# Recurrent-memory layer: another order of the model dimension, a fold of fewer products, output heads in column pieces, and a last step without queries

## The chip, the cores and the metric

The kernel runs on one core of one Trainium2 chip. The metric is the device time of one execution of the program in microseconds, as the median of several runs.

The core's engines work side by side, each through its own queue in a fixed order: TensorE (PE; its weight loads are shown as PEld), VectorE (DVE), ScalarE (ACT), GpSimd (POOL) and SyncE (SP), whose queue issues the DMA transfers here. An engine waits for another through semaphores.

## The reference

The prompt is 2048 tokens of 640 features. Four layers run one after the other, A, B, A, B, each with a layer norm before it and its result added to the residual x. Layer A is attention in four segments of 512 tokens with a linear memory (32 heads of 20). Layer B is a recurrent memory transformer with 32 heads of 128: 64 segments of 32 tokens, each with 8 memory tokens ahead of it.

```python
def _B_ref(x, mem0, Wq, Wk, Wv, Wo, seg_len):
    B, S, Dm = x.shape                 # 1, 2048, 640
...
    mask = (idx[:, None] < M) | (idx[:, None] >= idx[None, :])
    mem = mem0
    outs = []
    for s in range(n_seg):
        xs = x[:, s * seg_len:(s + 1) * seg_len, :].copy()
        h = jnp.concatenate([mem, xs], axis=1)
        q = jnp.einsum('btd,dhe->bhte', h, Wq)
        k = jnp.einsum('btd,dhe->bhte', h, Wk)
        v = jnp.einsum('btd,dhe->bhte', h, Wv)
        scores = jnp.einsum('bhqe,bhke->bhqk', q, k) * scale
        scores = jnp.where(mask[None, None], scores, -1000000000.0)
        p = _softmax(scores, axis=-1)
        o = jnp.einsum('bhqk,bhke->bhqe', p, v)
        o = jnp.einsum('bhte,hed->btd', o, Wo)
        mem = o[:, :M, :].copy()
        outs.append(o[:, M:, :])
    return jnp.concatenate(outs, axis=1)
...
x = A_x
x = x + _A_ref(_layernorm(x, axis=-1), A_wq, A_wk, A_wv, A_wo, A_beta)
x = x + _B_ref(_layernorm(x, axis=-1), B_mem0, B_Wq, B_Wk, B_Wv, B_Wo, B_seg_len)
x = x + _A_ref(_layernorm(x, axis=-1), A_wq, A_wk, A_wv, A_wo, A_beta)
x = x + _B_ref(_layernorm(x, axis=-1), B_mem0, B_Wq, B_Wk, B_Wv, B_Wo, B_seg_len)
return x
```

The memory of a segment is the output of the eight memory tokens of the segment before, so the 64 segments of a layer B are a chain. The eight memory rows that the last segment puts out are not returned.

## The kernel before

The residual lies in DRAM twice: in f32 (`xres`) and rounded to bf16 (`xres_bf`, from which layer B's layer norms read). The weights of layer B stay in SBUF with the model dimension on the 128 partitions in five chunks of 128 rows: `b_wq` and `b_wk` for the whole program, `b_wv` and `b_wo` for a layer.

Layer A (`layer_A`) goes through four segments of four 128-token tiles. The last thing it does for a tile is to store the new residual (L380), to round it (`a_xnb`; L383 on ACT in the last segment, L385 on POOL in the others) and to store that (L386). The first step's work of the next layer B, its layer norms and its first tail units, follows.

Layer B (`layer_B`) runs the 64 segments as steps. Every instruction of TensorE, ScalarE, VectorE and GpSimd is recorded through a helper, so that the profile shows L109 for all of them, and each engine keeps the order in which the program is written. A step has 32 columns that depend on the chain, eight memory rows and the first 24 tokens of the next segment, in the tile `HX` (`cols_of`); the eight last tokens of the segments, the tails, are worked off ahead of their steps in larger pieces, as filler between the chain's pieces. A step s does, in this order:

- `thin_mm`: the projections `b_Ka`, `b_Qa`, `b_Kb`, `b_Qb` (a and b are halves of the heads) of the 32 columns. The 32 columns are the stationary operand; four column groups of 32 of the PE array run at once, each on 512 other columns of the weight, five chunks deep. So a projection is 20 matmuls. Their results go to `b_kq` (ACT and DVE).
- `transp4` (`b_TPak`, `b_TPaq`, `b_TPbk`, `b_TPbq`) turns them, and they are scattered to the tiles `KT` and `QT`: the memory's part to those of this step, the part of the 24 tokens to those of the next.
- `mask_mm` and `scores` to `b_SP`, softmax on DVE and ACT (and POOL for one half), and turns of P on DVE. Under it PE does `b_Va` and `b_Vb`, a layer norm's transposes when one is due, and a unit of tail projections (`tail_unit`, `b_tail`). In the last steps of a layer that have no tail left, the unit is a repetition whose result is not used.
- `pv`: P times V to `b_OTP`, evicted to `b_OTsb` by ACT and DVE.
- `od_chunk(0)`: half of a chunk of deferred output heads of the tails (`b_OPSd`), then the output heads of the step with `o_mm` to `b_OPS`: the four column groups hold two heads times two halves of the 640 output columns, 320 columns each. That makes 16 rounds of four matmuls, in groups of two rounds by the list `order`. Then `od_chunk(1)`.
- the fold, which brings the memory rows from `b_OPS` to the memory columns of `HX` that the next projections use. ACT copies `b_OPS` to `b_msb` in three parts (64, 128, 128 columns); for each part PE multiplies slices of 32 columns of `b_msb`, as the stationary operand, with the constant `b_sel` (`selm`, 8 columns), which picks the memory rows, adds the two heads' groups and turns them (`b_MT`); DVE copies `b_MT` to `HX`. Between the parts lie chunks of `b_vtail` (`vtail_some`), values of tails of later steps, five chunks of four matmuls of 256 columns in a step.
- `x_out`: DVE adds `b_OPS` to the residual rows `b_XO`, and SP stores them (`store_head`, L1052). The residual rows were loaded at the step's start (L1102). The tails' residual (`b_XOd`, and `b_XOe` for the last four steps) is loaded and stored by `tail_dma` (L1063, L1061).

For the fold, a half jj of the output columns holds, of each chunk of 128 columns of the model dimension, the 64 columns of that half (`wo_half`, `d_half`):

```python
def wo_half(h, jj2):
    return W.wo[:, h, :].rearrange("p (c j x) -> p j c x", j=2, x=64)[:, jj2]

def d_half(rows, jj2):
    return rows.rearrange("t (c j x) -> t j c x", j=2, x=64)[:, jj2]
```

so that a chunk c of the next projections needs the columns 64c to 64c+63 of `b_OPS` in all four groups. One chunk takes four products, one for each column group of the result, over two slices of 32 columns and the two heads' halves of `b_sel`. The loads and stores of residual rows move pieces of 64 columns, 256 bytes, by the same rule.

The lines that the change and the prediction touch, besides these: L228 loads a weight of the next layer A (`a_wkv`) from its copy in DRAM; L760 and L765 load `b_wq`, `b_wk` and `b_wv`; L999 loads the first memory.

Of the kernel before, what the change touches and what calls it, by code (L numbers as in the profile page):

```python
# [18 lines left out]
F32 = mybir.dt.float32  # L19
# [10 lines left out]
NCH = 5  # L30
# [215 lines left out]
def layer_A(nc, tc, C, W, x_src, x_dst, src_is_bf16, nseg=4, out_bf16=False, xb_dst=None, load_w=None, side_loads=None):  # L246
# [7 lines left out]
    with ExitStack() as ctx:  # L254
# [105 lines left out]
        def out_stage_b(n_, tt, halves=(0, 1)):  # L360
            d = SEG[n_]
            oT, xr = d["oT"][tt], d["xr"][tt]
            r0 = n_ * 512 + tt * 128
            if xr is None:
                xr = wkl.tile([128, D], BF16 if src_is_bf16 else F32, name="a_xr")
                nc.sync.dma_start(xr[:], x_src[r0:r0 + 128, :])
            if n_ == nseg - 1 and (tt or not src_is_bf16):
                d["xnew"] = up.tile([128, D], F32, name="a_xnew", tag="PT") if tt else xr
            elif 0 in halves:
                d["xnew"] = w1l.tile([128, D], F32, name="a_xnew") if src_is_bf16 else xr  # L370
            xnew = d["xnew"]
            for half in halves:
                YP = pg.tile([128, 320], F32, name="a_YP", tag="pg")
                for c in range(NCH):
                    nc.tensor.matmul(YP[:], lhsT=oT[:, c, :], rhs=W.wo[:, c, 320 * half:320 * half + 320],
                                     start=(c == 0), stop=(c == NCH - 1))
                C.after2 = K("xnew").vector.tensor_tensor(out=xnew[:, 320 * half:320 * half + 320], in0=YP[:], in1=xr[:, 320 * half:320 * half + 320], op=ALU.add)
            if 1 not in halves:
                return
            nc.sync.dma_start(x_dst[r0:r0 + 128, :], xnew[:])  # L380
            xnb = w1l.tile([128, D], BF16, name="a_xnb")
            if n_ == nseg - 1:
                nc.scalar.copy(xnb[:], xnew[:])  # L383
            else:
                K("xnb").gpsimd.tensor_copy(xnb[:], xnew[:])  # L385
            nc.sync.dma_start(xb_dst[r0:r0 + 128, :], xnb[:])  # L386

        GS = {}
# [362 lines left out]
    return W  # L751


def load_B_resident(nc, W, B_Wq, B_Wk, k, after):

    c, r = divmod(k, 8)
    t, src = ((W.wk, B_Wk), (W.wq, B_Wq))[r % 2]
    h = r // 2
    nc.gpsimd.tensor_copy(t[0:1, c, 1024 * h:1024 * h + 1], after[0:1, 0:1])
    nc.sync.dma_start(t[:, c, 1024 * h:1024 * h + 1024], src[128 * c:128 * c + 128, 8 * h:8 * h + 8].rearrange("p h e -> p (h e)"))  # L760


def load_B_wv(nc, W, B_Wv):
    for c in range(NCH):
        nc.sync.dma_start(W.wv[:, c, :], B_Wv[128 * c:128 * c + 128].rearrange("p h e -> p (h e)"))  # L765


def load_B_wo(nc, W, B_Wo, k):
# [9 lines left out]
def layer_B(nc, tc, C, W, x_src, xb_src, x_dst, mem0, B_Wv, B_Wo, nsteps=64, out_bf16=False, tag=""):  # L778
# [8 lines left out]
    with ExitStack() as ctx:  # L787
# [21 lines left out]
        def ps_tile(shape, dtype, name):  # L809
            return pp.tile(shape, dtype, name=name, tag="ps")  # L810
# [68 lines left out]
        def thin_mm(cols_ap, Wt, b, name):  # L879
            ps = ps_tile([128, 512], F32, name)  # L880
            for c in range(NCH):
                for j in range(4):
                    n = 4 * b + j
                    nc.tensor.matmul(ps[32 * j:32 * j + 32, :], lhsT=cols_ap[:, c, :], rhs=Wt[:, c, 512 * n:512 * n + 512],
                                     start=(c == 0), stop=(c == NCH - 1), tile_position=(0, 32 * j), skip_group_check=True)
            return ps

        def transp4(sb, name, tp=None):
            if tp is None:
                tp = ps_tile([128, 4, 128], BF16, name)  # L890
            for i in range(4):
                nc.tensor.transpose(tp[:, i, :], sb[:, 128 * i:128 * i + 128], C.identb[:])
            return tp
# [76 lines left out]
                dma(VTd[8 * T:8 * T + 8, :, o:o + 256].rearrange("s t f -> (s t) f"), vt[64 * jj:64 * jj + 64])  # L970

        def wo_half(h, jj2):
            return W.wo[:, h, :].rearrange("p (c j x) -> p j c x", j=2, x=64)[:, jj2]

        def d_half(rows, jj2):
            return rows.rearrange("t (c j x) -> t j c x", j=2, x=64)[:, jj2]

        def o_mm(ops_, src_ap_fn, hpairs, first, last):
            for n_, h0 in enumerate(hpairs):
                for e in range(2):  # L980
                    for jj2 in range(2):
                        k = 2 * e + jj2
                        nc.tensor.matmul(ops_[32 * k:32 * k + 32, :].rearrange("p (c x) -> p c x", x=64), lhsT=src_ap_fn(h0 + e), rhs=wo_half(h0 + e, jj2),
                                         start=(first and n_ == 0), stop=(last and n_ == len(hpairs) - 1),
                                         tile_position=(0, 32 * k), skip_group_check=True)

# [9 lines left out]
        nc.gpsimd.memset(HX[0][:, :, 0, 0:8], 0.0)  # L996
        with nc.allow_non_contiguous_dma(reason="mem0 transpose load (tiny)"):
            for c in range(NCH):
                nc.sync.dma_start(HX[0][:, c, 1, 0:8], mem0[:, 128 * c:128 * c + 128].rearrange("t p -> p t"))  # L999
        tu_homes = ((kqp, "kq"),) * 4 + ((w2, "QT"), (w2, "KT"), (wk, "tu"), (w2, "Vth"))  # L1000
        for k in range(16):
            tail_unit(0, k, shared=True)
# [46 lines left out]
        def store_head(s):  # L1049
            def f(xo):  # L1050
                for jj2 in range(2):
                    nc.sync.dma_start(d_half(x_dst[32 * s:32 * s + 24, :], jj2), xo[32 * jj2:32 * jj2 + 24, :].rearrange("t (c x) -> t c x", x=64))  # L1052
            return f

        def tail_dma(s0, store, xo):
            x_ = x_dst if store else x_src
            for jj2 in range(2):
                sb = xo[32 * jj2:32 * jj2 + 32, :].rearrange("t (c x) -> t c x", x=64)
                dr = x_[32 * s0:32 * s0 + 128, :].rearrange("(i t) (c j x) -> i t j c x", t=32, j=2, x=64)[:, 24:32, jj2]
                if store:  # L1060
                    nc.sync.dma_start(dr, sb)  # L1061
                else:
                    nc.sync.dma_start(sb, dr)  # L1063
# [25 lines left out]
        for s in range(nsteps):  # L1089
# [9 lines left out]
                if s % 2:  # L1099
                    tl = tails_load(s + 1)  # L1100
            for jj2 in range(2):
                nc.sync.dma_start(XO[32 * jj2:32 * jj2 + 24, :].rearrange("t (c x) -> t c x", x=64), d_half(x_src[32 * s:32 * s + 24, :], jj2))  # L1102

            def x_scatter(tp, b, D_):
                if not last:
# [57 lines left out]

            Ka = thin_mm(cols, W.wk, 0, "b_Ka")
            ka = kq(Ka, "act")
            Qa = thin_mm(cols, W.wq, 0, "b_Qa")
            qa = kq(Qa, "dve", SCB)
            Kb = thin_mm(cols, W.wk, 1, "b_Kb")
            kb = kq(Kb, "act")
            Qb = thin_mm(cols, W.wq, 1, "b_Qb")  # L1170
            qb = kq(Qb, "act", SCB)

            TPak = transp4(ka, "b_TPak")
            scatter("dve", TPak, 0, KT[s], 0, 8, 32)
            x_scatter(TPak, 0, KT)
            TPaq = transp4(qa, "b_TPaq")
            scatter("dve", TPaq, 0, QT[s], 0, 8, 24)
            x_scatter(TPaq, 0, QT)
# [4 lines left out]
            TPbq = transp4(qb, "b_TPbq", po.tile([128, 4, 128], BF16, name="b_TPbq", tag="tail"))  # L1183
            scatter("dve", TPbq, 1, QT[s], 0, 8, 24)
            x_scatter(TPbq, 1, QT)
            SPb = mask_mm(1)
            scores((SPa, SPb))
            for f in (soft_max, soft_sub, soft_exp):
# [190 lines left out]
```

## Time and profile before

| | |
|---|---|
| runs, us | 2589.53, 2586.01, 2582.91 (median 2586.01) |
| the profiled execution: its time, us | 2585.25 |
| its span, first to last instruction, us | 2583.5 |
| granted TensorE clock | 0.996 |
| the two layers B, 63 steps each, us | 885.3 and 882.6 |
| period of a step, median, us | 13.98 |
| a projection of 20 matmuls, us | 1.08 |
| `b_OPS`, 64 matmuls, us | 2.17 |
| last rounds of `b_OPS` to the next `b_Ka`, median, us | 1.18 |
| ACT copy `b_msb` of 64 and 128 columns, mean ns | 213 (first part), 277 |

The page's busy times say how long an engine worked in the whole span. The chain of waits goes back from the last instruction to what released each, and its shares say on which engine the end hung. "issue" is time in which an engine waited for nothing that the profile shows. Matmuls are pipelined: in the timeline a group's time includes the overlap with the next one, and a round's cost is read from the distance of the starts. A line of the timeline gives start, time, engine, line, operation, output and inputs, the tile's shape and the count; in brackets stand the idle time of the engine before it and what ended it.

### The profile page before, as it was taken

To read this page: it belongs to the slowest core of one execution; us is meant where nothing else is said; L and a number is where in the kernel's file an instruction comes from. 1 tells how busy PE (TensorE), PEld (TensorE's weight loads), DVE (VectorE), ACT (ScalarE), POOL (GpSimd) and SP (SyncE) were. 2 spreads that over 40 slices of the span, in tenths; PEclk is the share of its full clock that TensorE was granted. 3 is DMA by queue.
4 is the path that set the end of the run, shared out by engine and by line. 5 is a ranking of instruction groups with operands and counts; after the bars stand their busy time and mean duration, and the time that the engine had idled before them with its cause. 6 is when DMAs were issued, how large, how long until landed. Compare 5 with 4: busy or idle time off the path is not lost.

```text
span 2583.5 us, 139561 instructions
## 1 busy us (share of the span) xinstructions
PE 2482.8 (96%) x62024; PEld 1637.5 (63%) x62088; DVE 1704.5 (66%) x4738; ACT 1521.3 (59%) x3430; POOL 704.9 (27%) x1515
## 2 busy tenths in 40 slices
PE   7999999999999999999979899999999999999998
PEld 5556576666666666666655566766666666666665
DVE  8999855565556555555579998555655565565555
ACT  6988945555555545444369889455555555555443
POOL 6677621111111111111146776211111111111110
PEclk9999999999999999999999999999999999999999
DMA  4122272222222222121220112822212122211111
GB/s 158 45 84 73 83 245 51 48 47 46 46 50 48 46 50 43 40 39 30 61 85 17 63 50 55 265 47 47 44 42 47 42 46 43 46 43 35 38 26 21
DMA packets 325309, 157.19 MB, mean 61 GB/s; under 512 B 244960, under 2 KB 309600, under 8 KB 322912
## 3 DMA queue, kind: packets, MB, share of 16 engines
q1 hardware_dynamic: 324704, 148.26, 22.1%
q8 instruction: 485, 7.95, 1.3%
q14 instruction: 120, 0.98, 0.1%
HBM read 96.46 MB, written 51.71 MB: 57 GB/s over the span
## 4 chain that ended last, share of the span: by engine, by line
PE 77%; DVE 14%; ACT 6%; issue 2%; DMA 1%; POOL 0%; SPq 0%; ACTq 0%; DVEq 0%; POOLq 0%
PE b_OPS L109 11%; DVE a_nm L138 6%; PE b_Ka L109 5%; PE b_Qb L109 5%; PE b_Kb L109 5%; PE b_Qa L109 5%; PE b_tail L109 5%; PE b_SP L109 4%; PE b_Va L109 4%; PE b_Vb L109 4%; PE b_vtail L109 3%; PE b_OPSd L109 3%; ACT a_PT L138 3%; PE b_OTP L109 3%; PE a_S L109 2%
## 5 line engine op out<-in xcount | busy, mean ns | idle before, releaser
L109 PEld LDWEIGHTS <-b_HX 128*32 128x32 bf16 x15360 | 428.7, 96 | 329.5 <-DVE b_HX L109 0.5
L109 POOL TENSOR_TENSOR b_Pn<-b_E,b_rs 128x200 bf16<-128x200 bf16 x128 | 78.2, 611 | 1334.4 <-PE b_Vb L109 893.7
L138 DVE TENSOR_REDUCE a_nm<-a_S 128x2 f32<-128x512 f32 (+3 forms) x512 | 395.0, 816 | 34.7 <-PE a_S L109 26.4
L138 ACT ACTIVATE a_PT<-a_T 128x1024 bf16<-128x1024 f32 (+1 forms) x384 | 344.3, 901 | 32.8 <-PE a_T L109 25.0
L109 PE MATMUL b_OPS<-b_wo,b_OTsb 128*32 128x320 bf16 x8192 | 302.4, 299 | 1.8 <-issue 0.8
L109 PEld LDWEIGHTS <-b_OTsb 128*32 128x32 bf16 x8192 | 204.4, 96 | 77.2 <-DVE b_OTsb L109 3.1
L138 POOL TENSOR_SCALAR_AFFINE_SELECT a_PT<-a_PT 128x256 bf16<-128x256 bf16 x380 | 188.6, 505 | 129.8 <-ACT a_PT L138 128.4
L109 DVE CAST b_HX<-b_MT 128x8 bf16<-128x8 f32 x372 | 63.9, 172 | 232.3 <-PE b_MT L109 226.6
L109 ACT CAST b_msb<-b_OPS 128x64 bf16<-128x64 f32 x378 | 69.4, 256 | 222.1 <-PE b_OPS L109 222.0
L109 ACT CAST b_kq<-b_Kb 128x512 bf16<-128x512 f32 x128 | 75.0, 586 | 200.4 <-PE b_Kb L109 200.4
L109 DVE COPY b_KT<-b_TPak 128x128 bf16<-128x128 bf16 x128 | 28.8, 225 | 228.1 <-PE b_TPak L109 228.1
L109 DVE TENSOR_SCALAR b_kq<-b_Qa 128x512 bf16<-128x512 f32 x128 | 88.6, 692 | 120.0 <-PE b_Qa L109 116.7
L109 PE MATMUL b_Va<-b_wv,b_HX 128*32 128x512 bf16 x2520 | 161.1, 380 | 0.0
L109 PE MATMUL b_Vb<-b_wv,b_HX 128*32 128x512 bf16 x2520 | 160.9, 379 | 0.0
L109 PEld LDWEIGHTS <-b_kq 128*128 128x128 bf16 x2080 | 116.8, 98 | 68.9 <-ACT b_kq L109 55.6
L109 PE MATMUL b_Ka<-b_wk,b_HX 128*32 128x512 bf16 x2520 | 158.3, 378 | 0.0
L109 PE MATMUL b_Qa<-b_wq,b_HX 128*32 128x512 bf16 x2520 | 158.2, 379 | 0.0
L109 PE MATMUL b_Qb<-b_wq,b_HX 128*32 128x512 bf16 x2520 | 158.2, 379 | 0.0
L109 PE MATMUL b_Kb<-b_wk,b_HX 128*32 128x512 bf16 x2520 | 158.2, 379 | 0.0
L109 DVE CAST b_OTsb<-b_OTP 128x160 bf16<-128x160 f32 (+1 forms) x384 | 131.0, 377 | 35.0 <-PE b_OTP L109 28.9
L109 PEld LDWEIGHTS <-c_identb 128*128 128x128 bf16 x1240 | 102.2, 98 | 60.1 <-issue 29.4
L109 ACT CAST b_kq<-b_Ka 128x512 bf16<-128x512 f32 x128 | 75.0, 586 | 108.8 <-PE b_Ka L109 108.8
(206 smaller groups left out, 5502.4 us busy)
## 6 DMA issues: line engine op xcount, KB each, us to landing
b_QKd<-b_tu SPq DMA_DIRECT2D x128, 128.0 KB
b_tl<-b_QKd SPq DMA_DIRECT2D x64, 256.0 KB
b_wv<-in_B_Wv_dram SPq DMA_DIRECT2D x10, 1024.0 KB
b_wo<-in_B_Wo_dram SPq DMA_DIRECT2D x16, 640.0 KB
b_Vth<-b_VTd SPq DMA_DIRECT2D x512, 16.0 KB
b_XO<-xres SPq DMA_DIRECT2D x256, 30.0 KB
b_VTd<-b_vt SPq DMA_DIRECT2D x224, 32.0 KB
b_xt<-xres_bf SPq DMA_DIRECT2D x40, 160.0 KB
```

Source lines behind the costliest of these rows:

```text
L109: r = f(*a, **k)
L138: r = f(*a, **k)
```

## The change

Layer B keeps the model dimension in another order. Chunks 0 to 3 take 128 rows each: chunk c takes the rows 320 (c mod 2) + 128 (c div 2) and the following; chunk 4 takes the rows 256 to 319 and 576 to 639. The weights `b_wq`, `b_wk` and `b_wv` and the first memory are loaded in this order, and layer A writes `xres_bf` in it, with two copies to `a_xnb` (512 and 128 columns) for the one there was: both on POOL, and in the last segment one on ACT and one on DVE. The halves of the output columns thereby become contiguous, 0 to 319 and 320 to 639, in `b_wo` and in the loads and stores of residual rows.

With this order the 128 columns of a part of `b_msb` serve two chunks, one for each half. A product takes a slice of 32 columns and all 16 columns of `b_sel`, and gives eight memory columns for either chunk. The parts are 128, 128 and 64 columns wide (64, 128, 128 before); there are 4 + 4 + 4 products (4 + 8 + 8 before), the last four with 8 columns. One chunk of `b_vtail` stands ahead of them (two before), two behind the first group (one before).

The last group of `b_OPS` is computed in two column pieces, 0 to 127 and 128 to 319: 8 + 8 matmuls for 8.

In the last step of a layer B the memory tokens' queries, whose outputs nobody reads, are left out: no `b_Qa`, `b_Qb`, no `b_TPaq`, `b_TPbq`, and POOL sets those columns of `QT` to zero.

```diff
@@ layer_A
             xnb = w1l.tile([128, D], BF16, name="a_xnb")
-            if n_ == nseg - 1:
-                nc.scalar.copy(xnb[:], xnew[:])
-            else:
-                K("xnb").gpsimd.tensor_copy(xnb[:], xnew[:])
+            halves_ = xnew[:].rearrange("p (j x) -> p j x", j=2)
+            moves = ((xnb[:, 0:512].rearrange("p (b j k) -> p b j k", b=2, j=2), halves_[:, :, 0:256].rearrange("p j (b k) -> p b j k", b=2)),
+                     (xnb[:, 512:640].rearrange("p (j k) -> p j k", j=2), halves_[:, :, 256:320]))
+            for (dst, src), last_ in zip(moves, (nc.scalar.copy, nc.vector.tensor_copy)):
+                (last_ if n_ == nseg - 1 else K("xnb").gpsimd.tensor_copy)(dst, src)
             nc.sync.dma_start(xb_dst[r0:r0 + 128, :], xnb[:])
@@
+def b_rows(src, c):
+
+    if c == 4:
+        return src.rearrange("(j k) h e -> j k h e", k=320)[:, 256:320]
+    o = 320 * (c % 2) + 128 * (c // 2)
+    return src[o:o + 128]
@@ load_B_resident, load_B_wv
-    nc.sync.dma_start(t[:, c, 1024 * h:1024 * h + 1024], src[128 * c:128 * c + 128, 8 * h:8 * h + 8].rearrange("p h e -> p (h e)"))
+    nc.sync.dma_start(t[:, c, 1024 * h:1024 * h + 1024], b_rows(src, c)[..., 8 * h:8 * h + 8, :].rearrange("... h e -> ... (h e)"))
-        nc.sync.dma_start(W.wv[:, c, :], B_Wv[128 * c:128 * c + 128].rearrange("p h e -> p (h e)"))
+        nc.sync.dma_start(W.wv[:, c, :], b_rows(B_Wv, c).rearrange("... h e -> ... (h e)"))
@@ layer_B
         def wo_half(h, jj2):
-            return W.wo[:, h, :].rearrange("p (c j x) -> p j c x", j=2, x=64)[:, jj2]
+            return W.wo[:, h, 320 * jj2:320 * jj2 + 320]
         def d_half(rows, jj2):
-            return rows.rearrange("t (c j x) -> t j c x", j=2, x=64)[:, jj2]
-        def o_mm(ops_, src_ap_fn, hpairs, first, last):
+            return rows[:, 320 * jj2:320 * jj2 + 320]
+        def o_mm(ops_, src_ap_fn, hpairs, first, last, c0=0, c1=320):
...
-                        nc.tensor.matmul(ops_[32 * k:32 * k + 32, :].rearrange("p (c x) -> p c x", x=64), lhsT=src_ap_fn(h0 + e), rhs=wo_half(h0 + e, jj2),
+                        nc.tensor.matmul(ops_[32 * k:32 * k + 32, c0:c1], lhsT=src_ap_fn(h0 + e), rhs=wo_half(h0 + e, jj2)[:, c0:c1],
@@ first memory
-                nc.sync.dma_start(HX[0][:, c, 1, 0:8], mem0[:, 128 * c:128 * c + 128].rearrange("t p -> p t"))
+                for p0, n_ in ((0, 64), (64, 64)) if c == 4 else ((0, 128),):
+                    o = 256 + 5 * p0 if c == 4 else 320 * (c % 2) + 128 * (c // 2)
+                    nc.sync.dma_start(HX[0][p0:p0 + n_, c, 1, 0:8], mem0[:, o:o + n_].rearrange("t p -> p t"))
@@ tail_dma; store_head and the load of b_XO likewise
-                sb = xo[32 * jj2:32 * jj2 + 32, :].rearrange("t (c x) -> t c x", x=64)
-                dr = x_[32 * s0:32 * s0 + 128, :].rearrange("(i t) (c j x) -> i t j c x", t=32, j=2, x=64)[:, 24:32, jj2]
+                sb = xo[32 * jj2:32 * jj2 + 32, :]
+                dr = x_[32 * s0:32 * s0 + 128, :].rearrange("(i t) d -> i t d", t=32)[:, 24:32, 320 * jj2:320 * jj2 + 320]
@@ a step
-            Qa = thin_mm(cols, W.wq, 0, "b_Qa")
-            qa = kq(Qa, "dve", SCB)
+            if not last:
+                Qa = thin_mm(cols, W.wq, 0, "b_Qa")
+                qa = kq(Qa, "dve", SCB)
...
-            Qb = thin_mm(cols, W.wq, 1, "b_Qb")
-            qb = kq(Qb, "act", SCB)
+            if last:
+                nc.gpsimd.memset(QT[s][:, :, 24:32], 0.0)
+            else:
+                Qb = thin_mm(cols, W.wq, 1, "b_Qb")
+                qb = kq(Qb, "act", SCB)
...
-                o_mm(ops, lambda h: OTsb[:, 40 * h + 8:40 * h + 40], [16 * a + 4 * j + 2 * ip for ip in range(2)], n_ == 0, n_ == 7)
+                for c0, c1 in ((0, 128), (128, 320)) if n_ == 7 else ((0, 320),):
+                    o_mm(ops, lambda h: OTsb[:, 40 * h + 8:40 * h + 40], [16 * a + 4 * j + 2 * ip for ip in range(2)], n_ == 0, n_ == 7, c0, c1)
...
-            vtail_some(2)
+            vtail_some(1)
...
-                parts = ((0, 1), (1, 3), (3, NCH))
+                parts = ((0, 128), (128, 256), (256, 320))
                 for ca, cb in parts:
-                    nc.scalar.copy(msb[:, 64 * ca:64 * cb], ops[:, 64 * ca:64 * cb])
+                    nc.scalar.copy(msb[:, ca:cb], ops[:, ca:cb])
                 for pi, (ca, cb) in enumerate(parts):
-                    mt = ps_tile([128, cb - ca, 8], F32, f"b_MT{pi}")
-                    for c in range(ca, cb):
-                        for q in range(4):
-                            o = 64 * c + 32 * (q % 2)
-                            nc.tensor.matmul(mt[32 * q:32 * q + 32, c - ca, :], lhsT=msb[:, o:o + 32], rhs=selm[:, q // 2, :],
-                                             start=True, stop=True, tile_position=(0, 32 * q), skip_group_check=True)
-                    nc.vector.tensor_copy(dst[:, ca:cb, 0:8], mt[:])
-                    vtail_some((1, 1, NCH)[pi])
+                    mt = ps_tile([128, 2, 8] if pi < 2 else [128, 8], F32, f"b_MT{pi}")
+                    for q in range(4):
+                        o = ca + 32 * q if pi < 2 else ca + 32 * (q % 2)
+                        nc.tensor.matmul(mt[32 * q:32 * q + 32], lhsT=msb[:, o:o + 32], rhs=selm[:] if pi < 2 else selm[:, q // 2, :],
+                                         start=True, stop=True, tile_position=(0, 32 * q), skip_group_check=True)
+                    nc.vector.tensor_copy(dst[:, 2 * pi:2 * pi + 2, 0:8] if pi < 2 else dst[:, 4, 0:8], mt[:])
+                    vtail_some((2, 1, NCH)[pi])
```

More of the change, by code (lines that the diff above doesn't have):

```diff
@@ L1051, in f @@
                 for jj2 in range(2):
-                    nc.sync.dma_start(d_half(x_dst[32 * s:32 * s + 24, :], jj2), xo[32 * jj2:32 * jj2 + 24, :].rearrange("t (c x) -> t c x", x=64))
+                    nc.sync.dma_start(d_half(x_dst[32 * s:32 * s + 24, :], jj2), xo[32 * jj2:32 * jj2 + 24, :])
             return f
@@ L1101, in layer_B @@
             for jj2 in range(2):
-                nc.sync.dma_start(XO[32 * jj2:32 * jj2 + 24, :].rearrange("t (c x) -> t c x", x=64), d_half(x_src[32 * s:32 * s + 24, :], jj2))
+                nc.sync.dma_start(XO[32 * jj2:32 * jj2 + 24, :], d_half(x_src[32 * s:32 * s + 24, :], jj2))
             def x_scatter(tp, b, D_):
@@ L1175, in layer_B @@
             x_scatter(TPak, 0, KT)
-            TPaq = transp4(qa, "b_TPaq")
-            scatter("dve", TPaq, 0, QT[s], 0, 8, 24)
-            x_scatter(TPaq, 0, QT)
+            if not last:
+                TPaq = transp4(qa, "b_TPaq")
+                scatter("dve", TPaq, 0, QT[s], 0, 8, 24)
+                x_scatter(TPaq, 0, QT)
             TPbk = transp4(kb, "b_TPbk")
@@ L1182, in layer_B @@
             SPa = mask_mm(0)
-            TPbq = transp4(qb, "b_TPbq", po.tile([128, 4, 128], BF16, name="b_TPbq", tag="tail"))
-            scatter("dve", TPbq, 1, QT[s], 0, 8, 24)
-            x_scatter(TPbq, 1, QT)
+            if not last:
+                TPbq = transp4(qb, "b_TPbq", po.tile([128, 4, 128], BF16, name="b_TPbq", tag="tail"))
+                scatter("dve", TPbq, 1, QT[s], 0, 8, 24)
+                x_scatter(TPbq, 1, QT)
             SPb = mask_mm(1)
```

## The prediction

> **What bounds the kernel now.** I read the page's busy times first, then the chain that ended last, then the timeline of one fold, then the chain at the ends of the layers.
>
> ```profile
> PE 2482.8 (96%) x62024; PEld 1637.5 (63%) x62088; DVE 1704.5 (66%) x4738; ACT 1521.3 (59%) x3430; POOL 704.9 (27%) x1515
> ...
> PE 77%; DVE 14%; ACT 6%; issue 2%; DMA 1%; POOL 0%; SPq 0%; ACTq 0%; DVEq 0%; POOLq 0%
> ```
>
> PE sets the pace: 96% busy and 77% of the chain. DMA is 1% of the chain, and in the steps of layer B (403 to 1270 us) no engine of the step waits for a transfer; so the wider runs of the residual loads and stores save nothing there. Of the 126 steps with a fold the median period is 13.98 us, and a fold looks like this (start, time of the group, engine, instruction):
>
> ```profile
> 837.70 0.44 PE L109 MATMUL b_OPSd<-b_wo,b_OTdef 128*32 128x320 bf16 x8
> 837.97 0.39 PE L109 MATMUL b_vtail<-b_wv,b_TX 128*32 128x256 bf16 x8
> 837.98 0.55 ACT L109 CAST b_msb<-b_OPS 128x64 bf16<-128x64 f32 x3 [1.76 <-PE b_OPS L109]
> 838.25 0.10 PEld L109 LDWEIGHTS <-b_msb 128*32 128x32 bf16 x4 [0.16 <-ACT b_msb L109]
> 838.25 0.19 PE L109 MATMUL b_MT<-b_sel,b_msb 128*32 128x8 bf16 x4
> 838.29 0.28 PE L109 MATMUL b_vtail<-b_wv,b_TX 128*32 128x256 bf16 x4
> 838.41 0.21 PE L109 MATMUL b_MT<-b_sel,b_msb 128*32 128x8 bf16 x8
> 838.48 0.28 PE L109 MATMUL b_vtail<-b_wv,b_TX 128*32 128x256 bf16 x4
> 838.59 0.21 PE L109 MATMUL b_MT<-b_sel,b_msb 128*32 128x8 bf16 x8
> 838.65 0.28 PE L109 MATMUL b_vtail<-b_wv,b_TX 128*32 128x256 bf16 x4
> 838.76 0.39 PE L109 MATMUL b_Ka<-b_wk,b_HX 128*32 128x512 bf16 x4
> ```
>
> Four matmuls in the four column groups run as one round; from start to start a round takes 136 ns at 320 columns, 109 at 256, 216 at 512, 44 at 40 (scores). The last rounds of b_OPS end at 837.87; ACT starts the first copy 0.11 later (837.98); 0.05 after that copy's end the products b_MT start. Meanwhile PE does two rounds of b_OPSd and two chunks of b_vtail, done at 837.97 + 2 x 0.109 = 838.19: it stands for 0.06 us until 838.25. From then to b_Ka everything is on PE's path.
>
> The ends of the layers (chain of waits; first the end of the first layer B, then the end of the kernel):
>
> ```profile
> 1295.78 0.50 DVE b_XOe L109
> 1296.31 0.64 SPq L1061
> 1296.98 0.62 SPq L1061
> 1297.65 7.38 DMA a_wkv<-a_wkv_home
> 1305.07 2.86 PE a_KV L109 x20
> ```
>
> ```profile
> 2561.11 1.08 PE b_Ka L109 x20
> 2562.19 1.08 PE b_Qa L109 x19
> 2563.27 1.08 PE b_Kb L109 x19
> 2564.35 1.08 PE b_Qb L109 x19
> 2565.43 0.33 PE b_TPak L109 x4
> ```
>
> In the first the next layer waits for its weights, whose load is issued behind two stores of the tail on SP's queue; in the second the four projections of the last step lie in a row on the path.
>
> **The change, part by part.** Sums are on the profiled execution (span 2583.5, its time 2585.25 us); the median of the runs, 2586.01, is 0.76 above that, added at the end.
>
> *The split of the last group.* Eight matmuls of 320 columns (two rounds, 272 ns) become two rounds of 128 and two of 192. By the slope of the wide rounds (216 - 109 over 256 columns, 0.42 ns per column) these take 56 and 83 ns: 278 in all, so b_OPS ends 6 ns later. The built program signals b_OPS once only, behind the last matmul of 192 columns, and the first msb copy waits for that count. The split therefore lets no copy start earlier.
>
> *The first copy.* It was 64 columns wide (213 ns in the fold); it becomes 128 (the second copy of that width takes 277, the nearest copy that stands first takes 266). +54 ns before the first product. On the clock of the fold above: b_OPS ends 837.878, copy 837.985 to 838.251, products from 838.303.
>
> *The cover.* One chunk of b_vtail before the products instead of two: PE is through with b_OPSd and that chunk at 837.706 + 0.272 + 0.109 = 838.087 and stands 0.216 us, not 0.06. The chunk is moved behind the products: four chunks there, 4 x 109 = 436 ns, not 327.
>
> *The products.* Five rounds (4 + 8 + 8) become three. A round that comes first in its group takes 40 ns, a second 25: 3 x 40 + 2 x 25 = 170 becomes 120, if one of 16 columns takes what one of 8 takes (both are far under the 40 columns of a scores round, 44 ns). A small wait before the second group (0.02 us) goes, since two chunks, 218 ns, now cover the second copy. The HX copies on DVE (172 ns) become three of 16, 16 and 8 columns, still behind chunks of b_vtail. If that cover went, up to 0.17 us a step would be bare.
>
> Sum for the step: b_Ka at 838.303 + 0.120 + 0.436 = 838.86 instead of 838.76; +0.101 us (0.086 to 0.116 by the copy's width price and the small wait). x 126 = **+12.7 us** (10.8 to 14.6). In about 12 steps PE already pauses 0.2 to 0.8 us (no releaser seen) between b_OPS and the products; the longer wait swallows some 0.12 of each: **-1.5** (-2 to 0).
>
> *The last step.* b_Qa and b_Qb (2 x 1.08) and two transposes (0.22 + 0.30) go; what was behind them is laid bare in part: b_kq of Kb is evicted by ACT (586 ns) with nothing but b_TPak over it. From b_Ka to b_Va 6.19 us becomes 4.11: **-2.1** at the kernel's end (-2.3 to -1.8). The memset of the query columns runs on POOL, idle there.
>
> *First layer B to A.* The same 2.1, and in the built program the a_wkv load stands ahead of the last tail stores on SP. It then waits for neither b_XOe nor the two issues (0.50 + 0.64 + 0.62 in the chain): issued at about 1292.8 instead of 1297.65. **-5.0** (-5.5, to -2.1 if another transfer binds).
>
> *The stores at the end.* Runs of 1280 B in place of five of 256 B; issue of the interleaved stores 0.64 to 0.84 us, of contiguous ones 0.32. Four such stores, two in the chain: **-1.2** (-2 to 0).
>
> *Layer A's xnb.* One copy of 640 columns on POOL (718 ns) becomes two (512 and 128). The nearest small cast takes 302, so +0.18 us each for 24: 4.4 us on an engine 27% busy, behind DVE's softmax. In the last segment ACT's copy gets shorter (0.73 in the chain, some 0.15 off) but DVE takes 128 columns in its own queue, and they wait for the previous xnb store's landing (4.06 us in the chain): behind them stand the next half's normalisation and b_tu, for which b_tail waits. Bounds: -0.5, and +2 if one landing is half exposed. I take **+0.5**, since most of the wait lies under the layer norms.
>
> The loads of weights and the six loads of mem0 (was five) lie under layer A's first segments: 0 (up to +0.3 if bare at the start).
>
> **Sum:** 12.7 - 1.5 - 2.1 - 5.0 - 1.2 + 0.5 = +3.4; 2585.25 + 3.4 + 0.76 = 2589.4, say **2590**. Own range by the bounds: 2584 to 2595.
>
> **Rivals.**
> 1. *The copy starts behind the first piece* (faster). Were the first 128 columns released by themselves, the copy would start some 0.165 us earlier and the stand be gone: -0.064 us a step, -8.1; with the ends -8.1 - 2.1 - 5.0 - 1.2 + 0.5 = -15.9: 2570. For it: the diff's column order. Against: the single signal in the build.
> 2. *The ends give nothing* (slower). The a_wkv load turns out to share its time with other loads and lands when it did; the stores' landing (2.16 us), not their issue, is what ends the kernel; DVE waits for one store. 12.7 - 1.5 - 2.1 + 2 = +11.1: 2597. It decides from about 4 us of lost gain. For it: 7.38 us for a load says that the queue is loaded there; against: it ran behind two stores.
> 3. *Narrow rounds have a fixed price* (slower). A 40-column round takes 44 ns where the slope gives 17: 27 ns that, if every round bears them, two added rounds pay: +54 instead of +6, 6.0 us more: 2596. With the weight load (96 ns, four to a round) as the floor, 2603. For it: that row. Against: 256 columns at 109 and 320 at 136 leave no offset, so it looks like a floor under 100 columns.
>
> The Trainium skill ("TensorEngine Tiling (Array Packing)", section "Instruction Overhead") gives each matmul an overhead of about 60 cycles, and the same latency to one column as to sixty. Read as a floor, it makes the 16-column products as cheap as the 8-column ones, and the sum stands; read as an addition to each round, it is the third rival. The trace agrees with the floor: rounds of 256 and 320 columns lie on one line through zero.
>
> **How the numbers follow.** Forecast 0.58, first rival 0.13, second 0.19, third 0.10. A measurement of this kernel can tell about 0.3% (7.8 us) from no change: 2578.2 to 2593.8. The forecast falls within, the first rival below, the other two above: faster 0.13, same 0.58, slower 0.29. The range leaves out the first rival and the far end of the third: 2577 to 2600.
>
> **What would show it.** Right: the first b_msb copy 128 columns wide, 0.11 us behind the 192-column b_OPS; a wait of PE for ACT b_msb of about 0.22 us ahead of the products, some 27 us over all steps; the median period 14.08; in the last step 4.1 us from b_Ka to b_Va; a_KV of the second A about 5 us nearer to the last step's fold. Wrong: a first copy that starts ahead of the last b_OPS rounds (rival 1); a_KV still behind a_wkv at the old distance (2); 128-column rounds of 80 ns and more (3). The prediction is wrong as a whole if the step doesn't lose, or loses over 0.15 us.

## The result and the profile after

The changed kernel takes 2608.07 us (median of 6 runs, 2604.83 to 2612.5), the kernel before 2585.89 beside it: ratio 1.0087, 95% interval 1.0074 to 1.0100, about 22 us slower. Forecast were 2590 and a range up to 2600.

Where the time went is seen when the span is cut at the first b_Ka of each layer B and at the b_Ka of its last step. The third and fourth columns are two of the kernels of the experiments below (one profile each; profiles of kernels with the same steps differ by up to 5 us in a layer):

| us | before | after | after, fifth chunk in two loads | the fastest |
|---|---|---|---|---|
| start to the first b_Ka | 389.3 | 407.3 | 387.9 | 387.5 |
| first layer B, 63 steps | 885.3 | 888.0 | 888.8 | 881.7 |
| its last step, second layer A, to the next first b_Ka | 403.8 | 410.2 | 393.5 | 396.3 |
| second layer B, 63 steps | 882.6 | 884.5 | 887.6 | 882.8 |
| last step to the end | 22.6 | 18.9 | 19.1 | 19.1 |
| span | 2583.5 | 2608.9 | 2576.9 | 2567.5 |

In these profiles the 126 steps lost 4.6 us, which is within that scatter, and the end won 3.7. The rest, +18.0 and +6.5, lies in the stretches that hold the two layers A, where the forecast had a gain. The page's busy times hardly moved:

```profile
PE 2481.8 (95%) x61944; PEld 1642.1 (63%) x62008; DVE 1695.7 (65%) x4740; ACT 1520.1 (58%) x3428; POOL 708.0 (27%) x1541
```

PE works as much as before and the span is 25 us longer, so PE stands idle. The waits of the changed kernel from 335 to 376 us, the end of the first layer A (who waits for whom: us, times, longest):

```profile
ACT a_xnb L386 <- DVE a_xnew L138: 14.0, 1, 14.0
DVE b_ln_st L109 <- DMA b_xt<-xres_bf: 12.3, 1, 12.3
PE a_YP L109 <- DVE a_xnew L138: 12.3, 1, 12.3
```

The three are one wait. DVE has b_ln_st of layer B ahead of a_xnew in its queue, b_ln_st waits 12.3 us for the load of b_xt, and PE and ACT wait for a_xnew behind it. At the same place in the second layer A DVE waits 14.5 us; in the kernel before neither wait exists. On SP's queue the last load of b_wv, its fifth chunk, stands just ahead of the first load of b_xt:

```profile
333.80 0.55 SPq L774 DMA_DIRECT2D b_wv<-in_B_Wv_dram  x1
335.74 0.33 SPq L387 DMA_DIRECT2D xres_bf<-a_xnb  x1
336.11 0.58 SPq L859 DMA_DIRECT2D b_xt<-xres_bf  x1
```

What the transfers were doing meanwhile is in the table by windows (window, its length, busy time of PE, PEld, DVE, ACT and POOL with counts, then granted clock, DMA share, GB/s):

```profile
340.00:345.00 5.00, 5.00 (x83) 3.75 (x82) 3.53 (x10) 3.50 (x5) 0.78 (x2) 1.00 0.28 92
345.00:350.00 5.00, 1.96 (x16) 1.22 (x15) 0.63 (x2) 0.77 (x4) 0.00 (x0) 1.00 0.20 74
350.00:355.00 5.00, 0.00 (x0) 0.00 (x0) 0.00 (x0) 0.00 (x0) 0.00 (x0) 0.63 0.13 54
355.00:360.00 5.00, 0.24 (x2) 0.12 (x2) 1.70 (x6) 0.00 (x0) 0.55 (x1) 0.50 0.09 34
360.00:365.00 5.00, 5.00 (x23) 3.02 (x22) 3.31 (x10) 1.31 (x2) 0.63 (x2) 0.50 0.48 166
365.00:370.00 5.00, 5.00 (x73) 4.50 (x72) 2.73 (x9) 1.70 (x3) 0.00 (x0) 1.00 0.57 198
```

From 350 to 355 no engine does anything, and the DMA share is 0.13 at 54 GB/s: 0.13 of 16 is two engines. The records of that stretch are packets of 8 KB, one row of b_wv, 0.31 us each, 13 in 2 us. The fifth chunk of b_wv, 128 rows from two places, is one transfer with the dimensions (2, 64, 4096). On two engines its 128 packets take 64 x 0.31 = 19.8 us. The b_xt loads behind it on the queue land when these two are through: of packets of 1,280 B, the size of a row of `xres_bf`, 89 start from 345 to 350, none from 350 to 355, and 80 from 356 to 361. The pause has a price behind it, too: the granted clock falls to 0.50 and stays there until 365.

The fold after, in the timeline of one step:

```profile
857.08 0.44 PE L109 MATMUL b_OPSd<-b_wo,b_OTdef 128*32 128x320 bf16 x8
857.35 0.28 PE L109 MATMUL b_vtail<-b_wv,b_TX 128*32 128x256 bf16 x4
857.36 0.55 ACT L109 CAST b_msb<-b_OPS 128x128 bf16<-128x128 f32 x3 [1.76 <-PE b_OPS L109]
857.68 0.10 PEld L109 LDWEIGHTS <-b_msb 128*32 128x32 bf16 x4 [0.35 <-ACT b_msb L109]
857.68 0.19 PE L109 MATMUL b_MT<-b_sel,b_msb 128*32 128x16 bf16 x4
857.72 0.39 PE L109 MATMUL b_vtail<-b_wv,b_TX 128*32 128x256 bf16 x8
...
858.23 0.39 PE L109 MATMUL b_Ka<-b_wk,b_HX 128*32 128x512 bf16 x4
```

One chunk of b_vtail is through at 857.35 + 0.11 = 857.46 and the products (`b_MT`) start at 857.68: PE stands 0.22 us, the number forecast.

And the end of the first layer B, in the chain of waits:

```profile
1295.51 1.08 PE b_Ka L109 x20
1296.59 1.11 PE b_Kb L109 x20
...
1312.47 0.36 SPq L1063
1312.87 6.86 DMA a_wkv<-a_wkv_home
1319.78 2.02 PE a_KV L109 x20
```

From b_Ka to a_KV 24.4 us, where before it was 30.5 (b_Ka at 1274.59, a_KV at 1305.07).

### The profile page after: what moved, and what is told of

The parts are those of the page before. It is cut to its first block, busy times and chain, and to the rows that moved or that the text cites. A ratio compares the mean times of both kernels' runs of the same rounds, so it can differ in the third digit from the quotient of the medians.

```text
span 2608.9 us, 139430 instructions
## 1 busy us (share of the span) xinstructions
PE 2481.8 (95%) x61944; PEld 1642.1 (63%) x62008; DVE 1695.7 (65%) x4740; ACT 1520.1 (58%) x3428; POOL 708.0 (27%) x1541
## 4 chain that ended last, share of the span: by engine, by line
PE 46%; DVE 5%; ACT 4%; DMA 2%; issue 1%; POOL 0%; SPq 0%; ACTq 0%; DVEq 0%
PE b_OPS L109 7%; PE b_tail L109 4%; PE b_Ka L109 3%; PE b_Kb L109 3%; PE b_Va L109 3%; PE b_Qb L109 3%; PE b_Qa L109 3%; PE b_Vb L109 3%; DVE a_nm L138 2%; PE b_SP L109 2%; PE b_vtail L109 2%; PE b_OTP L109 2%; ACT a_PT L138 2%; PE b_OPSd L109 1%; PE a_S L109 1%; PE b_TPak L109 1%
## 5 line engine op out<-in xcount | busy, mean ns | idle before, releaser
L109 PEld LDWEIGHTS <-b_HX 128*32 128x32 bf16 x15360 | 434.4, 96 | 325.7 <-issue 0.7
L109 PE MATMUL b_OPS<-b_wo,b_OTsb 128*32 128x320 bf16 (+1 forms) x9216 | 304.4, 284 | 6.2 <-issue 5.0
L109 PEld LDWEIGHTS <-b_OTsb 128*32 128x32 bf16 x9216 | 218.8, 96 | 82.9 <-issue 7.5
L109 DVE CAST b_HX<-b_MT 128x16 bf16<-128x16 f32 x372 | 59.2, 172 | 247.3 <-PE b_MT L109 234.3
L109 ACT CAST b_msb<-b_OPS 128x128 bf16<-128x128 f32 x378 | 69.5, 256 | 228.6 <-PE b_OPS L109 228.6
```

Source lines behind the costliest of these rows:

```text
L109: r = f(*a, **k)
```

## The experiments

### The loads of the fifth chunk

The first runs put theory L (two DMA engines) against rival X (the two copies of a_xnb). In the changed kernel, the fifth chunk of all three weights is loaded in two transfers of 64 rows; the cut shows b_wv:

```diff
+def b_parts(c):
+    if c == 4:
+        return ((0, 64, 256), (64, 128, 576))
+    return ((0, 128, 320 * (c % 2) + 128 * (c // 2)),)
...
-        nc.sync.dma_start(W.wv[:, c, :], b_rows(B_Wv, c).rearrange("... h e -> ... (h e)"))
+        for p0, p1, o in b_parts(c):
+            nc.sync.dma_start(W.wv[p0:p1, c, :], B_Wv[o:o + p1 - p0].rearrange("p h e -> p (h e)"))
```

> The changed kernel, but the fifth chunk of b_wq, b_wk and b_wv (rows 256 to 319 and 576 to 639) is loaded by two transfers of 64 rows instead of one whose outermost dimension has two blocks. Theory L (the two-block transfer is carried by two of the 16 DMA engines, some 53 GB/s, and the loads of b_xt queue behind it, for which DVE waits 12.3 and 14.5 us): both waits go, and a 2.5 us wait of DVE for a store in the first layer A too; the first b_Ka comes near 390 us instead of 407, and of 2608.1 about 28 us go: 2580. Rival X (the second copy of a_xnb, put into DVE's queue in the last segment of A and onto POOL in the others, is what holds the next layer up): nothing changes, 2608.

Measured 2578.64 us, ratio to before 0.9966 (0.9954 to 0.9978). The first b_Ka is at 387.9, and of the waits of DVE for b_xt 0.3 us is left, in the second layer. Theory L holds; the change turns from slower to faster by this edit alone.

The same for b_wv only:

> The same for b_wv alone; b_wq and b_wk keep the two-block transfers (eight of 256 KB in the first layer A). Theory L: the two long waits go, the 2.5 us wait for the store in the first layer A stays: 2582 to 2583, some 2.5 above the run with all loads split. Rival X: 2608.

2580.10 us, 0.9967 (0.9952 to 0.9982). The 2.6 us wait of DVE for a store is still there in the profile, and a wait of 3.2 us for b_xt in the second layer; the long ones are gone. The times don't separate the two runs.

The other direction, two blocks in the kernel before:

```diff
+        src = B_Wv[128 * c:128 * c + 128].rearrange("p h e -> p (h e)")
-        nc.sync.dma_start(W.wv[:, c, :], B_Wv[128 * c:128 * c + 128].rearrange("p h e -> p (h e)"))
+        nc.sync.dma_start(W.wv[:, c, :], src if c < 4 else B_Wv[512:640].rearrange("(j k) h e -> j k h e", j=2).rearrange("... h e -> ... (h e)"))
```

> The kernel before, its fifth chunk of b_wv (rows 512 to 639, one contiguous range) written as two blocks of 64 rows in one transfer; nothing else is changed. Theory L: 25 to 28 us slower than before, 2611 to 2614, with DVE waiting 12 to 15 us for b_xt at the end of either layer A. Rival X: as before, 2586. If the transfer's two blocks are merged when they lie next to each other: also 2586, and the DMA share then shows no stretch at 0.1.

2586.67 us, 0.9996 (0.9987 to 1.0006), and no wait for b_xt. This fits the case, named beforehand, in which adjoining blocks are merged, so the run doesn't decide on L. The next run has blocks that don't adjoin:

```diff
+        src = B_Wv[128 * c:128 * c + 128]
+        if c == 4:
+            src = B_Wv.rearrange("(j k) h e -> j k h e", k=320)[:, 256:320]
```

> The kernel before, with one change: the fifth chunk of b_wv is loaded in one transfer from the rows 256 to 319 and 576 to 639, two blocks that don't lie next to each other (so that they can't be merged, as two adjoining blocks could be). The weights of this chunk are then not those of the reference's rows; no instruction's size or order changes. Theory L: some 25 us slower, 2611, a stretch of the DMA share at 0.1 and about 53 GB/s ahead of the b_ln_st of either layer B, and DVE waits for b_xt by 12 to 15 us each time. Rival X: as before.

2619.58 us, 1.0117 (1.0097 to 1.0137), 30 us slower by nothing but that transfer. Its waits from 300 to 380 us and one window:

```profile
DVE b_ln_st L109 <- DMA b_xt<-xres_bf: 13.4, 1, 13.4
```

```profile
350.00:355.00 5.00, 0.00 (x0) 0.00 (x0) 0.00 (x0) 0.00 (x0) 0.00 (x0) 0.50 0.13 52
```

The second layer has 14.7. So the form of the load is enough to make the loss, and taking it away undoes the loss. With four blocks of 32 rows (k=160, rows 128 to 159 of each):

> The kernel before, the fifth chunk of b_wv loaded in one transfer from four blocks of 32 rows with gaps between them (the weights of this chunk are again not those of the reference's rows). Theory L in its strict form (the outermost dimension's blocks are dealt out to as many DMA engines): 128 packets of 8 KB at 0.31 us each are over in 9.9 us on four engines, where two need 19.8; the waits for b_xt are 2 to 5 us, 5 to 12 us slower than before in all, and the DMA share stands at 0.25 and about 105 GB/s for a while. Rival (a transfer from blocks with gaps is slow in itself, whatever their number): 30 us slower, as with two blocks.

2610.00 us, 1.0080 (1.0057 to 1.0103), some 21 us slower, between the 5 to 12 us of the strict form and the 30 us of the rival; DVE waits 9.2 us each time, not 2 to 5. A window in the first stall and one in the second:

```profile
345.00:350.00 5.00, 0.00 (x0) 0.00 (x0) 0.00 (x0) 0.00 (x0) 0.00 (x0) 0.81 0.25 76
1647.00:1651.00 4.00, 0.49 (x4) 0.21 (x3) 0.00 (x0) 0.00 (x0) 0.00 (x0) 1.00 0.25 95
```

0.25 of 16 is four engines, as the strict form says. The rate is 76 GB/s in the first stall, where a packet of 8 KB takes 0.43 us in the mean, and 95 in the second, where the median packet takes 0.31. So the number of engines follows the number of blocks, but a packet's time isn't fixed: over the whole of the first transfer its median is 0.60 us, and 0.58 from 335 to 340 us in the kernel with two loads. What slows the packets is open.

The Trainium skill ("DMA: Bandwidth & Descriptors", section "Rules for kernel authors") says it in a sentence: an outermost dimension of size c below 16 confines the whole transfer to at most c engines. The DMA shares of 0.13 and 0.25 agree.

Rival X by itself, two copies of a_xnb in the kernel before:

> The kernel before with a_xnb written by two copies (512 and 128 columns, the columns in their old order) on the engines of the changed kernel: POOL twice, in the last segment ACT and DVE. Theory L: within 2 us of before, 2584 to 2588. Rival X: some 25 us slower, 2610.

2584.13 us, 0.9991 (0.9982 to 1.0001). The copies cost nothing that can be measured (4.7 us less to 0.3 us more by the interval); rival X, 25 us, falls.

### The fold

All from the changed kernel with the fifth chunks in two loads (2578.64, ratio 0.9966). First the places of b_vtail:

```diff
-            vtail_some(1)
+            vtail_some(2)
...
-                    vtail_some((2, 1, NCH)[pi])
+                    vtail_some((1, 1, NCH)[pi])
```

> The changed kernel with all fifth chunks loaded in two transfers (2578.6), and the chunks of b_vtail in the old places: two ahead of the products, one behind each group of them. The theory of the fold (the first copy of 128 columns, begun behind the whole of b_OPS, makes PE stand about 0.16 us longer ahead of the products; what is moved ahead of them fills this): the stand goes to 0.1 us or less, b_Ka is then bound by the HX copy, some 0.47 us behind the first product, and comes 0.05 us earlier in a step: -6 to -7 us, 2572. Rival (the second copy isn't ready and PE stands there instead): no gain, 2578 to 2580.

2574.99 us, 0.9943 (0.9928 to 0.9958). From the last round of b_OPS to b_Ka the median falls from 1.197 to 1.148 us, as said; the difference of the two medians, 3.6 us, is smaller than the 6 of that sum, the ratios' gain of 0.0023 fits it. The intervals of the two ratios touch, so it is the stretch and not the time that shows the gain.

Three ahead, none behind the last products:

> As the run with two chunks of b_vtail ahead of the products, but three ahead, one behind the first and one behind the second group, none behind the third. The theory of the fold: PE doesn't stand ahead of the products any more, but some 0.1 us ahead of b_Ka, for the HX copy on DVE: -0.04 us a step, 2573, no better than two ahead. Rival (b_Ka doesn't wait for the HX copy): -0.15 us a step, 2560.

2578.48 us, 0.9958 (0.9944 to 0.9973). PE doesn't stand ahead of the products any more (a round of 0.10 us lies between) but ahead of b_Ka, 1.161 us behind the last round of b_OPS: not better than two, as the theory says, though the time is not the 2573 forecast. The rival's 2560 is out. By their times alone the runs with one, two and three chunks ahead can't be told apart.

The split of the last group undone:

```diff
-                for c0, c1 in ((0, 128), (128, 320)) if n_ == 7 else ((0, 320),):
+                for c0, c1 in ((0, 320),):
```

> The same kernel (all fifth chunks in two transfers, 2578.6) with the last group of b_OPS in one piece, 8 matmuls of 320 columns. The theory of the single signal (the first copy waits for the whole of b_OPS in either case): no difference, 2577 to 2580, and the time from the end of b_OPS to the copy stays 0.107 us. Rival (the pieces let the first copy begin earlier): +0.16 us a step, some 20 us slower, 2598.

2571.83 us, 0.9930 (0.9913 to 0.9946). Both expectations were wrong. The copy starts 0.107 us behind b_OPS in either kernel and the undisturbed step (the lower quartile of the 126 periods) is 13.892 us, not 13.899: on the path the split costs 0.007 us and lets nothing start earlier, as the single signal says. Yet the kernel is some 7 to 9 us faster without it. What differs in the two profiles is PE's pauses without a releaser inside b_OPS (starts more than 0.17 us apart): 14 with 8.4 us in all and a median of 0.56 us with the split, 17 with 5.4 us without. Of these 17, 13 aren't pauses: they are rounds 0.20 to 0.26 us apart in one step from 1679 to 1682 us, where the granted clock was at half (0.85 and 0.81 in the windows from 1675 to 1680 and 1685). That leaves 4 with 2.2 us, so the pauses make up some 6 of the 7 to 9 us. Other profiles agree: what the b_OPS of the 126 steps take above their tenth percentile adds up to 6.9 to 8.1 us in the five kernels with this split and to 2.1 to 4.5 in the eight without it.

Theory F says that PE stands where it uses up its instructions faster than the next ones arrive. It came from the DMA records: PE's instructions arrive as packets of 16 KB on the queue marked instruction, 485 in the kernel before for 62,024 + 62,088 = 124,112 instructions of PE and PEld, 256 to a packet, and no two start less than 3.3 us apart. The pauses of over 0.4 us inside the steps nearly all end 2.3 to 3.0 us behind such a start. A split adds instructions in b_OPS, where a step takes 128 in 2.2 us. So the first rival of the prediction was made real, the first 128 columns in a bank of their own in all 16 rounds, which puts the most instructions there:

```diff
+                opsA = po.tile([128, 128], F32, name="b_OPSA", tag="tail")
+                ops = po.tile([128, 192], F32, name="b_OPS", tag="ops")
+                pieces = ((opsA, 0, 128, 0), (ops, 128, 320, 128))
...
+                for t_, c0, c1, off in pieces:
+                    o_mm(t_, lambda h: OTsb[:, 40 * h + 8:40 * h + 40], [16 * a + 4 * j + 2 * ip for ip in range(2)], n_ == 0, n_ == 7, c0, c1, off)
...
+                    nc.scalar.copy(msb[:, ca:cb], opsA[:] if ca == 0 else ops[:, ca - 128:cb - 128])
```

> The changed kernel with all fifth chunks in two transfers (2578.6), and the first 128 columns of b_OPS in a tile and bank of their own (that of b_tail) in all 16 rounds, so that the first copy can begin behind their last round; x_out adds in two pieces. This is the first rival of the prediction made real. Theory P (only the path counts): the copy begins 0.17 us earlier, the products with it, and 14 more rounds in two pieces cost 3 ns each: -0.12 us a step, 2563. Theory F (PE's instructions come in packets of 16 KB, 256 instructions, on the queue marked instruction; where PE takes them faster than a packet lands, some 2.3 to 3 us after its start, it stands, as in the pauses without a releaser): a step's b_OPS takes 256 instructions instead of 144 in 2.2 us, so PE stands 0.3 us or more in most steps there: 2600 or more, and the pauses are seen inside b_OPS.

2719.95 us, 1.0493 (1.0476 to 1.0510). Theory F holds. One step of it in the timeline of PE:

```profile
807.67 0.28 PE L109 MATMUL b_OPSA<-b_wo,b_OTsb 128*32 128x128 bf16 x8
807.78 0.25 PE L109 MATMUL b_OPS<-b_wo,b_OTsb 128*32 128x192 bf16 x2
809.07 0.34 PE L109 MATMUL b_OPS<-b_wo,b_OTsb 128*32 128x192 bf16 x6 [1.04 <-issue]
809.17 0.30 PE L109 MATMUL b_OPSA<-b_wo,b_OTsb 128*32 128x128 bf16 x6
```

and its costliest groups on the page (busy, mean ns, then the idle time before them and its cause):

```profile
L109 PE MATMUL b_OPS<-b_wo,b_OTsb 128*32 128x192 bf16 x8192 | 302.3, 247 | 33.5 <-issue 33.4
L109 PE MATMUL b_OPSA<-b_wo,b_OTsb 128*32 128x128 bf16 x8064 | 288.5, 219 | 41.8 <-issue 40.3
```

PE stops in the middle of a round of four, between two matmuls that wait for nothing, for 1.0 us. The path itself did what theory P said: the first copy starts 0.06 us ahead of the end of b_OPS, and b_Ka comes 1.03 us behind the last round in the median step, where it was 1.20; the shortest tenth of the b_OPS takes up to 2.39 us, where it was 2.35. But PE pauses without a releaser for over 0.4 us (from start to start) 141 times, in 109 of the 126 steps; 137 of these pauses end 2.0 to 3.2 us behind the start of an instruction packet, where packets start 4.2 us apart on average. So the two layers B are 137 us longer (954.4 + 959.1 against 888.8 + 887.6). The Trainium skill ("Runtime: NRT & Kernel Launch", section "Instruction fetch mechanics") has the 16 KiB blocks of 256 instructions and calls the cost of crossing one mostly hidden. The trace agrees with the block (16 KB, 256 instructions) and not, for stretches like this, with hidden.

Both good edits together, the last group whole and two chunks ahead:

> The changed kernel with all fifth chunks in two transfers, the last group of b_OPS in one piece, and two chunks of b_vtail ahead of the products, one behind each group. If the gains of the two edits (3.6 and 6.7 us below 2578.6 where each was alone, or more) add up: 2566 to 2569. If both shorten the same wait: 2572. By theory F the pauses of PE inside b_OPS stay as few as with the whole last group.

2568.69 us, 0.9913 (0.9898 to 0.9927): the lowest time of all, 22 us below before in its own comparison. By the ratios the two gains add up within the noise: 0.0023 and 0.0036 alone, 0.0053 together. Its b_OPS has 5 pauses with 2.2 us. Its fold:

```profile
834.75 0.39 PE L109 MATMUL b_vtail<-b_wv,b_TX 128*32 128x256 bf16 x8
834.76 0.55 ACT L109 CAST b_msb<-b_OPS 128x128 bf16<-128x128 f32 x3 [1.76 <-PE b_OPS L109]
835.08 0.10 PEld L109 LDWEIGHTS <-b_msb 128*32 128x32 bf16 x4 [0.22 <-ACT b_msb L109]
...
835.55 0.40 PE L109 MATMUL b_Ka<-b_wk,b_HX 128*32 128x512 bf16 x4
```

Two chunks end at 834.97, so PE stands 0.11 us, and b_Ka comes 0.47 us behind the products' start (0.55 in the changed kernel).

### The last step

> The kernel before with one part of the change: the last step of either layer B without the memory tokens' queries. Theory: from b_Ka to b_Va of the last step 4.0 us instead of 6.19, either layer 2.1 us shorter at its end, and the layer between (whose weights' load then waits for nothing of the step) up to 5: 2582 to 2584 where before is 2588. Rival (the time between the layers is set by something else): 2586.

2585.77 us, 0.9982 (0.9973 to 0.9992). From b_Ka to b_Va 4.04 us; the end of the kernel falls from 22.6 to 19.7 us, and a_KV comes 1.7 us nearer to b_Ka (28.8 us). The time fell by some 4.7 us by the ratio, as forecast (4 to 6). The theory holds for the step; of the up to 5 us between the layers only 1.7 came: there the a_wkv load is still issued behind the b_XOe stores, 21.2 us behind b_Ka; in the changed kernel, where it stands ahead of them, it is 17.5.

## Why the prediction was wrong, point by point

**The step that failed** is the sentence "The loads of weights and the six loads of mem0 (was five) lie under layer A's first segments: 0 (up to +0.3 if bare at the start)". It put the loads at nothing and named a cover, but not how long the loads last or what stands behind them. The loads of b_wv are issued from 320 us on, in the last segment of layer A, the fifth straight ahead of the b_xt loads that open layer B; and no term allowed for a transfer longer than one of 128 contiguous rows. It runs on two engines, 19.8 us, and costs 29 to 31 us in all (2608.07 to 2578.64, or 1.0087 to 0.9966 of before; 30 by itself in the kernel before). The waits in the trace are 12.3, 14.5 and 2.5 us; PE's half clock after the two long ones comes on top. Everything needed was to be had: the new access pattern stands in the diff, its place in the queue in the profile, and the rule in the Trainium skill's page cited above.

The other steps can be read from the kernel with two loads, which is 2578.64 where the forecast was 2590. So without this loss the sum would still have had the wrong sign: +3.4 us were forecast, and by the ratio it is about 9 us faster than before. The steps lost less and the way from layer B to A won more than forecast:

- *The step, +0.101 us.* Right in kind, too large. The undisturbed step (the tenth percentile of the periods) grew from 13.82 to 13.90 us, 0.07. The stand of 0.22 us is as forecast, and so are the 0.42 us from the end of b_OPS to the first product; the stretch from there to b_Ka is 0.53 us, not 0.556, which is most of the miss. x 126 this is 9 us, not 12.7. The median period, forecast as 14.08, is 13.94 in the changed kernel and 13.99 in the one with two loads, where it was 13.98: the loss named as the sign doesn't show in the median.
- *Pauses absorbed, -1.5.* Right in kind, too small, and not the only such effect. What the 126 stretches from the end of b_OPS to the first product take above their tenth percentile is 3.1 to 5.5 us in the six profiles with the steps of the kernel before and 1.4 to 2.2 in the three with the changed steps, some 2.6 us less. By the same measure b_OPS gained some 4 us by the split, and the whole period fell from 26 to 33 us to 22 to 26. So the mean step is 14.03 to 14.08 us in the six profiles and 14.07 to 14.10 in the three: the steps lost some 2 us on average, within the scatter, and 11 were forecast. Why the other stretches had fewer pauses is open.
- *The split, 6 ns, no early copy.* Right on the path (0.007 us; 0.107 us from b_OPS to the copy). That it costs some 7 to 9 us otherwise, mostly by late instructions, was no step of the sum.
- *The last step, -2.1.* Right: 6.19 became 4.03.
- *First layer B to A, -5.0.* Right in kind, a little more than its bound of -5.5: a_KV is 6.0 us nearer. 1.7 are the queries'; the rest goes with the earlier place of the a_wkv load, which no run changed by itself.
- *The stores at the end, -1.2.* Of the right sign: the end fell by 3.7 with the last step, by 2.9 where only the queries were left out. The difference of 0.8 is hardly more than the scatter, 22.1 to 22.7 us in the kernels with the old end.
- *Layer A's xnb, +0.5.* No cost was seen: the two copies by themselves made -4.7 to +0.3 us by the interval.
- *The range.* The bounds of the terms, added up, reach from 2584 to 2599, not to 2595. The result lies outside either.

Of the rivals, the second said that the ends give nothing: they gave what was forecast or more, and another loss hid it. The first didn't occur and, made real, is slower. The third's place was right, its mechanism not: with all 16 rounds in two pieces the undisturbed b_OPS is only 0.04 us longer; the narrow rounds have no fixed price of the size named, they bring more instructions.

## What to carry to other kernels

Read a small outermost dimension of a transfer (2 and 4 here, blocks with gaps between them) as the number of engines that will carry it; when an edit permutes a layout, look at every load that it rewrites, at what it now has outermost, and at what is queued behind it. A load on a side path is free only until a small urgent one stands behind it. And count instructions where an engine's work is finest: a piece that starts something earlier can lose more in instruction supply than it wins on the path.

## What was not expected of the hardware

- A transfer of two separate blocks moved 51 to 54 GB/s on its own, one of four 76 in one stall and 95 in the other; two adjoining blocks cost nothing that can be measured.
- PE's instructions came in blocks of 256, no closer than 3.3 us. Stretches that use them faster stop in the middle of a round: the starts around the pauses of over 0.4 us lie up to 0.9 us apart in the steps of the kernel before, and up to 2.4 us, with a median of 1.2, with all 16 rounds in two pieces.
- In the first pause of the changed kernel PE's last matmul ends at 347.5 us. The granted clock is 1.00 until 351 and 0.50 from then to 365, while PE's work goes on from 359.8: for some 5 us PE worked at half the clock.
